# Linear attention and a gated feed-forward layer: turning the first chunks' keys and rows on TensorE, spreading the constants, halving the last store, and a new order

## The chip, the cores and the metric

The kernel runs on one core of one Trainium2 chip. The metric is the device time of one execution in microseconds (us); lower is better. The kernel before has a median of 525.44 us over three runs (525.37 to 525.9). The execution that the profiler recorded took 528.41 us, with 526.7 us between its first and its last instruction (its span). All rows below are from that execution.

Names used here: TensorE (PE in the profile, PEld for its weight loads) multiplies matrices; VectorE (DVE), ScalarE (ACT) and GpSimd (POOL) do elementwise work; SyncE (SP) issues nearly all DMA transfers. SBUF is the on-chip memory, PSUM the memory that TensorE writes.

## What is computed

For each of 4 batches and 8 heads, over 768 steps of 48 channels, in f32:

```python
for t in range(S):
    state = alpha[:, :, t, :, None] * state + np.einsum('bhd,bhe->bhde', k[:, :, t], v[:, :, t])
    y[:, :, t] = np.einsum('bhd,bhde->bhe', q[:, :, t], state)
```

The heads of a token are then laid side by side (3072 tokens of 384 numbers), and each token goes through a normalised, gated layer with d_ff = 1536:

```python
xn = x / np.sqrt(np.mean(x * x, axis=-1, keepdims=True) + 1e-06) * rms_g
g = xn @ w_gate
return ((g * (1.0 / (1.0 + np.exp(-g)))) * (xn @ w_val) @ w_out).astype(np.float32)
```

The weights arrive as 64-bit floats.

## The kernel before

**Splitting.** TensorE works on pairs of f16 numbers: each f32 operand is split into a high f16 part (ACT) and the remainder, the low part, also f16. A product is three matmuls, high by high, high by low and low by high (`SPLIT`, m = 0 to 2). The low part is made by DVE as a subtraction, or by TensorE, which subtracts the high part from a copy of the f32 value that lies in PSUM (a matmul with a matrix of -1 on the diagonal, `minus`), after which ACT copies the rest out. Which way is used for which chunk stands in the lists `LOW_A`, `LOW_X`, `LOW_K`, `LOW_V`, `LOW_W`.

**Chunks.** A chunk is 128 tokens of one batch; there are 24. Chunks 0 to 3 are the first of each batch. `attention(cc)` handles one: two scans on DVE (`scan`, L702) give the running decay, keys and queries are scaled by it (`kh`, `qp`, L720 and L725), TensorE forms the scores (L835 in f32 for the first chunks, L826 in f16 pairs for the others), DVE masks them (L841), they are split, and TensorE multiplies them with the values into `y` (L916). For the states the split keys are needed with tokens on the partitions, `kT`. The rows `y` are normalised with `rms_g` into `x`, split, and needed with channels on the partitions, `xT`.

**Turning.** Before, both turns are DMA transposes on the SP queue: `k_turn` (L736) and `x_turn` (L1013).

**Feed-forward.** The 24 chunks form the groups `GROUPS` = 4, 2, 2, 4, 4, 4, 4. For a group, `expert_in` runs over 12 tiles of 128 hidden units: 9 matmuls for the gate (`mm_f_c_0`) and 9 for the value (`mm_f_c_1`), all L1152; ACT takes the silu of the first, DVE multiplies (`h`, L1169), and the result is split (ACT, then DVE at L1182). `expert_out` (L1222) multiplies with `w_out`; DVE scales the result (L1236) and a store takes it out (L1240). For group 0 the first five hidden tiles are done with 256 columns, first for chunks 0 and 1 (`mm_f_0_*`), then for chunks 2 and 3 (`mm_f_2_*`), so that TensorE can begin before chunks 2 and 3 are normalised. The three PSUM buffers `mm` are shared by these products, the key products of chunks whose low part TensorE makes, and, for names in `BANK_M`, the weights that are decoded.

**Weights.** `decode` loads a weight tile of 64-bit floats into one of two buffers `raw`, and DVE and ACT make f32 words of it with integer operations (L525, L538, L530, L546, L557) and split them (ACT L562, DVE L565). For names in `LOW_W` the words are joined in PSUM in two halves (L578) and the low part is made by TensorE (L590) and ACT (L596).

**Order.** The program is not written in its order. Every step is an operation with a cost, an engine, its buffers and a due time; `Plan.order` places them with a simple model, and the tables `PACE`, `GAP`, `FIRST_DUE`, `AHEAD`, `STRIDE`, `LATE`, `NUDGE` and `HOLD` shift due times. Each engine then executes its own list strictly in that order.

**Constants.** Masks and diagonal matrices are made at the start by POOL (memset and affine_select).

## Time and profile before

| | us |
|---|---|
| median of three runs | 525.44 |
| the profiled execution | 528.41 |
| its span | 526.7 |
| PE busy | 501.4 |
| DVE busy | 401.5 |
| ACT busy | 277.2 |
| POOL busy | 27.1 |

Busy time is the union of an engine's instructions. Matmuls overlap, so the mean duration of one is longer than the distance between two. An instruction of DVE starts about 0.08 us before the one ahead of it has ended, so the sum of durations is a little more than the time they take. A wait is named by what released it. The clock of PE is given as the share of its full speed that was granted: 1.00 stands for 2.4 GHz, 0.50 for 1.2 GHz.

### The profile page before, as it was taken

The page shows a single profiled execution, that of the slowest core. Times are in us where ns is not written, and L with a number is a line of the kernel's source. Part 1 is how long each engine was busy: PE and PEld are TensorE (multiplying, and loading weights), DVE is VectorE, ACT ScalarE, POOL GpSimd, SP SyncE. Part 2 cuts the span into 40 slices and gives each one's busy share as a digit, 9 for nine tenths or more (in the row PEclk, how much of TensorE's full clock was granted, in tenths as well). Part 3 has the DMA queues.
Part 4 walks back from the last instruction along what each step waited for, and adds up shares of the span by engine and source line. Part 5 has one row for each costly group of instructions (what it writes and reads, how often), then busy time and mean ns, then how long its engine had stood idle before and what let it go on. Part 6 is the DMA issues. An engine that isn't in the chain of part 4 may idle for free.

```text
span 526.7 us, 11922 instructions
## 1 busy us (share of the span) xinstructions
PE 501.4 (95%) x4826; PEld 299.4 (57%) x4826; DVE 401.5 (76%) x755; ACT 277.2 (53%) x720; POOL 27.1 (5%) x61
## 2 busy tenths in 40 slices
PE   3768999999999999999999999999999999999995
PEld 2447744567877886444566445556544456444453
DVE  7999899999999999999988659999474631233330
ACT  3787776645554663546554567766575630233300
POOL 4001000010001000001100000101000000000000
PEclk9959899999999999999999999999999999999999
DMA  8989757437534245444267756525532201000000
GB/s 254 311 213 221 252 181 242 127 92 188 133 81 92 69 102 132 109 110 91 69 167 208 178 154 144 163 83 124 208 107 90 75 16 46 15 1 1 1 30 34
DMA packets 70669, 64.68 MB, mean 123 GB/s; under 512 B 39921, under 2 KB 64625, under 8 KB 70609
## 3 DMA queue, kind: packets, MB, share of 16 engines
q1 hardware_dynamic: 70464, 63.68, 45.1%
q8 instruction: 38, 0.62, 0.5%
q10 hardware_dynamic: 144, 0.20, 0.1%
q14 instruction: 23, 0.18, 0.1%
HBM read 49.84 MB, written 4.72 MB: 104 GB/s over the span
## 4 chain that ended last, share of the span: by engine, by line
PE 73%; DVE 16%; issue 2%; ACT 1%; DMA 1%; DVEq 0%
PE mm L1152 44%; PE mm_po L1222 21%; DVE dk L702 3%; PE at L826 2%; PE y L916 2%; PE y L906 2%; DVE h L1182 1%; DVE h L1169 1%; DMA xT<-x 1%; DVE at L841 1%; PE at L934 1%; DVE a L896 1%; DVE raw_o L530 1%; DVE wu_o L557 1%; DVE s L816 1%
## 5 line engine op out<-in xcount | busy, mean ns | idle before, releaser
L1152 PE MATMUL mm<-xT,wg 128*128 128x512 f16 (+1 forms) x1602 | 290.0, 340 | 2.5 <-DMA xT<-x 2.5
L1152 PEld LDWEIGHTS <-wg 128*128 128x128 f16 x1602 | 154.9, 98 | 122.9 <-issue 3.0
L1222 PE MATMUL mm_po<-wo,h 128*128 128x384 f16 x864 | 145.9, 326 | 1.1 <-DVE ob L1236 0.8
L1222 PEld LDWEIGHTS <-h 128*128 128x128 f16 x864 | 82.6, 98 | 55.5 <-issue 1.8
L1169 DVE SCALAR_TENSOR_TENSOR h<-mm,sl 128x512 f32<-128x512 f32 (+1 forms) x89 | 51.8, 582 | 44.3 <-PE mm L1152 42.7
L490 ACT ACTIVATE h<-h 128x512 f16<-128x512 f32 (+1 forms) x89 | 48.5, 545 | 68.1 <-DVE h L1169 67.6
L1163 ACT ACTIVATE sl<-mm 128x512 f32<-128x512 f32 (+1 forms) x89 | 45.4, 510 | 40.8 <-PE mm L1152 40.2
L1182 DVE TENSOR_TENSOR h<-h,h 128x512 f16<-128x512 f32 (+1 forms) x89 | 51.6, 581 | 17.7 <-ACT h L490 17.7
L702 DVE TENSOR_TENSOR_SCAN dk<-att,seed 112x520 f32<-112x520 f32 x48 | 60.5, 1260 | 2.5 <-DMA att<-att 2.0
L974 POOL TENSOR_TENSOR ss<-ss,mhalf 128x1 f32<-128x1 f32 x24 | 20.3, 846 | 400.9 <-DVE ss L964 355.0
L1236 DVE TENSOR_SCALAR ob<-mm_po 128x384 f32<-128x384 f32 x24 | 13.2, 551 | 31.5 <-PE mm_po L1222 31.5
L893 ACT CAST a<-at 128x512 f16<-128x512 f32 x48 | 27.6, 582 | 13.9 <-DVE at L841 13.4
L841 DVE TENSOR_TENSOR at<-at,mask 128x512 f32<-128x512 f32 x48 | 31.7, 691 | 0.7 <-PE at L835 0.5
L916 PE MATMUL y<-v,a 128*128 128x48 f16 x576 | 27.2, 186 | 0.1
L896 DVE TENSOR_TENSOR a<-at,a 128x512 f16<-128x512 f32 x38 | 25.1, 682 | 0.0
L645 ACT ACTIVATE wu_s<-wu_s 128x768 f32<-128x768 f32 x18 | 15.1, 840 | 15.6 <-DVE wu_s L641 15.6
L916 PEld LDWEIGHTS <-a 128*128 128x128 f16 x576 | 22.8, 98 | 0.4
L906 PE MATMUL y<-s,q 112*128 112x96 f16 x240 | 22.8, 204 | 0.0
L490 ACT ACTIVATE k<-kh 112x512 f16<-112x512 f32 x24 | 15.0, 625 | 11.6 <-DVE kh L720 8.9
L958 ACT ACTIVATE junk<-y 128x384 bf16<-128x384 f32 x24 | 11.7, 486 | 17.1 <-PE y L916 8.8
L826 PEld LDWEIGHTS <-k 48*128 48x128 f16 x480 | 13.5, 94 | 6.7 <-issue 6.3
L906 PEld LDWEIGHTS <-q 112*128 112x128 f16 x240 | 14.8, 96 | 4.1
(142 smaller groups left out, 447.9 us busy)
## 6 DMA issues: line engine op xcount, KB each, us to landing
att<-att SPq DMA_DIRECT2D x22, 675.9 KB, 5.7
v<-vtok SPq DMA_DIRECT2D x24, 192.0 KB, 3.9
raw_i<-w_gate SPq DMA_DIRECT2D x12, 384.0 KB, 4.4
raw_i<-w_val SPq DMA_DIRECT2D x12, 384.0 KB, 5.3
raw_o<-w_out SPq DMA_DIRECT2D x6, 768.0 KB, 4.9
raw_s<-w_gate SPq DMA_DIRECT2D x12, 384.0 KB, 3.6
raw_s<-w_val SPq DMA_DIRECT2D x12, 384.0 KB, 4.9
raw_s<-w_out SPq DMA_DIRECT2D x6, 768.0 KB, 4.6
```

Source lines behind the costliest of these rows:

```text
L490: nc.scalar.activation(dst, src, AF.Copy, scale=scale, accum_out=stat[:rows, col : col + 1])
L702: nc.vector.tensor_tensor_scan(out, x, start.rearrange("r g p c -> r (g p c)"), 0.0, op0=ALU.mult, op1=ALU.add)
L841: nc.vector.tensor_tensor(t["sc"][j], t["sc"][j], mask[:, int(not sc16)].to_broadcast([P, NP, C]), op=ALU.mult,)
L893: nc.scalar.copy(a_tile()[:, j, 0], t["sc"][j])
L896: nc.vector.tensor_tensor(a_tile()[:, j, 1], t["sc"][j], a_tile()[:, j, 0], op=ALU.subtract)
L906: nc.tensor.matmul(yps[:, 2 * p * D : 2 * (p + 1) * D], t["q16"][:, x, p, :], s16_tile()[:, y, p].rearrange("r j e -> r (j e)"), start=p = ...
L916: nc.tensor.matmul(yps[:, (2 * p + j) * D : (2 * p + j + 1) * D], a_tile()[:, j, x, p, :], t["v16"][:, y, p, j, :], start=first and p == 0 ...
L1152: nc.tensor.matmul(ps[:, :n], wg[:, f, x, j, kk, :], xT[:, y, kk, cs], start=i == 0, stop=i == 3 * NK - 1,)
L1163: nc.scalar.activation(t["sl"][:, :n], t[0][:, :n], AF.Silu, scale=1.0 / (S_X * S_W))
L1169: nc.vector.scalar_tensor_tensor(t["h"][:, :n], t[1][:, :n], S_H / (S_X * S_W), t["sl"][:, :n], op0=ALU.mult, op1=ALU.mult,)
L1182: nc.vector.tensor_tensor(h16_of(g, f)[:, 1, cs], t["h"][:, :n], h16_of(g, f)[:, 0, cs], op=ALU.subtract)
L1222: nc.tensor.matmul(t[i][:, :DM], h16_of(g, f)[:, x, ts], wo[:, f // 2, y, f % 2, :], start=f == 0 and m == 0, stop=f == NF - 1 and m == 2,)
```

## The change

For chunks 0 to 3 (`TURN_X`) the normalised rows are no longer split and then turned by a DMA transpose. DVE writes `x32`, TensorE turns it by three f32 matmuls against the identity `same` into the `y` bank (`x_bring`), ACT writes the high part straight into `xT`, and the low part comes from TensorE and ACT for chunks 0 and 1 (`LOW_X`) and from DVE for 2 and 3 (`xT_lo`). For chunks 0 to 2 (`TURN_K`, where scores are in f32) the keys are turned in the same way, by four f32 matmuls into an `mm` bank (`k_bring`), and the low part is made by TensorE and ACT. Chunk 3 is now in `SC16`: its scores are in f16 pairs, and its keys are split by DVE and turned by DMA, as before. The values of chunks 0 and 1 have their low part from DVE now, no longer from TensorE. The weight tile i1 joins `LOW_W`, and i1, i3 and i10 join `BANK_M`. POOL makes `minus` and two masks only; ACT derives `same`, `minus_w` and `plus_w` from `minus`; DVE clears `seed2`. The last store is in two halves of columns, one scaled by DVE and stored from SP, one scaled by ACT and stored from ACT. Costs and order tables are new, so all five lists differ.

```diff
-SC16 = []
+SC16 = [3]
-LOW_K = [0, 1]
-LOW_V = [0, 1]
-BANK_M = ["i0"]
+LOW_K = [0, 1, 2, 3]
+TURN_X = [0, 1, 2, 3]
+TURN_K = [0, 1, 2, 3]
+BANK_M = ["i0", "i1", "i3", "i10"]
-LOW_W = ["i0", "i6", "o1"]
+LOW_W = ["i0", "i1", "i6", "o1"]
...
-PACE = [0.932, 0.85, 1.174, 1.159, 0.85, 0.982, 1.687, 0.852]
+PACE = [0.973, 0.85, 1.174, 1.159, 0.85, 1.072, 1.687, 0.852]
...
-    nc.gpsimd.memset(seed2, 0.0)
+    nc.vector.memset(seed2, 0.0)
...
+    for x, scale in ((same, -1.0), (minus_w, 1.0 / S_W), (plus_w, -(2.0**128) / S_W)):
+        nc.scalar.activation(x, minus, AF.Copy, scale=scale)
...
         def k_bring():
-            t["kps"] = buf(ps_mm, [R, 512], F32, "mm", ("k", cc))
-            nc.tensor.matmul(
-                t["kps"], same[:R, :R], t["kh"].rearrange("r p c -> r (p c)"),
-                start=True, stop=False,
-            )
+            t["kps"] = buf(ps_mm, [P, 512], F32, "mm", ("k", cc))
+            for p in range(NP):
+                nc.tensor.matmul(
+                    t["kps"][:, p * R : (p + 1) * R], t["kh"][:, p, :], same[:R, :R],
+                    start=p == 0, stop=True, skip_group_check=True,
+                )
...
+        def gain_r():
+            t["x32"] = tl(ap, [P, DM], F32, "x32")
+            nc.vector.scalar_tensor_tensor(
+                t["x32"], t["y"][:, :DM], t["ss"][:, 3:4], rg, op0=ALU.mult, op1=ALU.mult
+            )
+
+        def x_bring():
+            for k in range(NK):
+                nc.tensor.matmul(
+                    t["y"][:, k * P : (k + 1) * P], t["x32"][:, k * P : (k + 1) * P], same,
+                    start=k == 0, stop=True, skip_group_check=True,
+                )
+
+        def xT_hi():
+            nc.scalar.copy(xT_part(0), xT_ps())
+
+        def xT_lo():
+            nc.vector.tensor_tensor(xT_part(1), xT_ps(), xT_part(0), op=ALU.subtract)
...
-        if cc in LOW_X:
-            xs = add("DVE", "xs", gain_at, [y1, rt, tiles["rg"]], [key("y"), key("ss")])
-            xd = add("ACT", "xh", x_hi_of, [xs], [key("y"), key("x16")])
-            xl = add("PE", "xless", x_less, [xd], [key("y"), key("x16")])
-            xl = add("ACT", "xr", x_rest, [xl], [key("y"), key("x16")])
+        if cc in TURN_X:
+            yk, xk = key("y"), ("xT", g)
+            x = add("DVE", "xs", gain_r, [y1, rt, tiles["rg"]], [yk, key("ss"), key("x32")])
+            xt = add("PE", "xid", x_bring, [x], [yk, key("x32")])
+            xt = add("ACT", "xh", xT_hi, [xt], [yk, xk])
+            if cc in LOW_X:
+                xt = add("PE", "xless", x_less, [xt], [yk, xk])
+                xt = add("ACT", "xr", x_rest, [xt], [yk, xk])
+            else:
+                xt = add("DVE", "xTl", xT_lo, [xt], [yk, xk])
...
             if ends(i):
-                op("ACT", 0.1, lambda i=i: store(i), [e], [o], due=now + 5)
+                for h, (e, q) in enumerate((("DVE", "SP"), ("ACT", "ACT"))):
+                    r = op(e, 0.3, lambda i=i, h=h: back(i, h), [tail[0]], [b, o], due=now + 2)
+                    op(q, 0.4, lambda i=i, h=h: store(i, h), [r], [o], due=now + 5)
```

POOL's list at the very start, before: `same`, `same_v`, `minus`, `minus_w` and `plus_w` are diagonal matrices.

```order
L446 AFFINE_SELECT mask<-mask 128x384
L459 MEMSET plus_w 128x128
L461 MEMSET minus_w 128x128
L463 AFFINE_SELECT minus<-minus 128x128
L463 AFFINE_SELECT minus_w<-minus_w 128x128
L463 AFFINE_SELECT plus_w<-plus_w 128x128
L463 AFFINE_SELECT same<-same 128x128
L463 AFFINE_SELECT same_v<-same_v 128x128
```

And POOL's list at the same place now, from `minus` on.

```order
L432 MEMSET minus 128x128
L440 MEMSET mask 64x128
L433 ISA
L433 AFFINE_SELECT minus<-minus 128x128
L441 MEMSET mask 64x128
L440 MEMSET mask 64x128
```

Six affine_selects have become two, the first of them earlier in the list.

DVE's list before, where chunk 3 is normalised (`x_3`); the first number in a name is the chunk, or for `h` group, hidden tile and chunk.

```order
L538 TENSOR_SCALAR wu_i_685<-raw_i_532 128x768
L978 TENSOR_TENSOR x_3_691<-y_594,rg 128x384
L707 RECIPROCAL seed_95<-dk_507 112x8
L1169 SCALAR_TENSOR_TENSOR h_0_0_0_706<-mm_0_0_1_642,sl_0_0_658 128x256
L1169 SCALAR_TENSOR_TENSOR h_0_1_0_708<-mm_1_0_1_675,sl_1_0_687 128x256
L546 SCALAR_TENSOR_TENSOR wu_i_685<-raw_i_532,wu_i_685 128x768
L1002 SCALAR_TENSOR_TENSOR x_3_710<-x_3_691,ss_655,x_3_710 128x384
```

And DVE's list now, where chunk 3 is normalised and the low parts of chunks 2 and 3 are written into `xT` (L969).

```order
L797 TENSOR_TENSOR sd_132<-st_131,gd_681 112x192
L537 SCALAR_TENSOR_TENSOR wu_i_749<-raw_i_581,wu_i_749 128x768
L810 TENSOR_TENSOR s_139<-sd_132,s_139 48x4x48
L948 SCALAR_TENSOR_TENSOR x_3_784<-y_598,ss_698,rg 128x384
L969 TENSOR_TENSOR xT_390<-y_502,xT_390 128x3x128
L556 SCALAR_TENSOR_TENSOR wg<-wu_i_749,wg 128x768
L810 TENSOR_TENSOR s_139<-sd_132,s_139 48x4x48
L529 TENSOR_SCALAR wu_i_805<-raw_i_713 128x768
L1149 SCALAR_TENSOR_TENSOR h_0_3_0_817<-mm_3_0_1_767,sl_3_0_762 128x256
L1162 TENSOR_TENSOR h_0_2_765<-h_0_2_0_753,h_0_2_765 128x256
L969 TENSOR_TENSOR xT_390<-y_598,xT_390 128x3x128
```

Before, the last row of chunk 3 is the 65th instruction of DVE after the first scan has begun, and a DMA follows; now it is the 81st, and the first gates `h` stand ahead of it in both.

DVE's list now a little earlier, between the decoding of two weight tiles and the first gate (`raw_i_408` holds i3, `raw_i_516` holds i4).

```order
L516 TENSOR_SCALAR raw_i_408<-raw_i_408 128x768
L521 SCALAR_TENSOR_TENSOR raw_i_408<-raw_i_408 128x768
L548 SCALAR_TENSOR_TENSOR wu_i_562<-raw_i_408 128x768
L693 SCALAR_TENSOR_TENSOR dk_578<-att_224,seed 112x520
L529 TENSOR_SCALAR wu_i_595<-raw_i_516 128x768
L556 SCALAR_TENSOR_TENSOR wg<-wu_i_562,wg 128x768
L698 RECIPROCAL seed_95<-dk_578 112x8
L1149 SCALAR_TENSOR_TENSOR h_0_0_0_677<-mm_0_0_1_568,sl_0_0_564 128x256
```

In both lists the first gate `h_0_0_0` stands behind the last step of i3 and the first step of i4; before, the first step of x_3 stood between them, and now the first scan of chunk 4 stands there instead, and the first steps of i3 directly ahead.

The SP queue before, from the first `xT` on.

```order
L1013 DMA_TRANSPOSE xT_476<-x_0_391 128x6x128
L1013 DMA_TRANSPOSE xT_476<-x_1_397 128x6x128
L736 DMA_TRANSPOSE kT_520<-k_2_494 128x8x112
L517 DMA raw_i_532<-w_gate 128x3x128
L517 DMA raw_i_532<-w_val 128x3x128
L517 DMA raw_i_637<-w_gate 128x3x128
L517 DMA raw_i_637<-w_val 128x3x128
L1013 DMA_TRANSPOSE xT_476<-x_2_592 128x6x128
```

The SP queue now, at the loads of i3 and i4.

```order
L508 DMA raw_i_408<-w_gate 128x3x128
L508 DMA raw_i_408<-w_val 128x3x128
L727 DMA_TRANSPOSE kT_468<-k_3_401 128x8x112
L508 DMA raw_i_516<-w_gate 128x3x128
L508 DMA raw_i_516<-w_val 128x3x128
L415 DMA v_544<-vtok 128x384
```

Of the eight transposes that chunks 0 to 3 sent through this queue one is left, the keys of chunk 3.

## Rows read from the trace of the kernel before

**Rows 1.** The page's part on engines: busy us, share of the span, instructions.

```profile
PE 501.4 (95%) x4826; PEld 299.4 (57%) x4826; DVE 401.5 (76%) x755; ACT 277.2 (53%) x720; POOL 27.1 (5%) x61
```

**Rows 2.** Busy time of each engine in stretches of the span: start and end, then length, PE, PEld, DVE, ACT and POOL busy with their instructions, the granted clock of PE, the share of the DMA engines and GB/s.

```profile
30.00:40.00 10.00, 6.70 (x153) 5.21 (x143) 9.96 (x16) 8.38 (x23) 0.72 (x1) 0.50 0.68 179
40.00:50.00 10.00, 10.00 (x135) 8.62 (x132) 9.87 (x21) 8.28 (x24) 2.20 (x1) 0.94 0.87 209
50.00:60.00 10.00, 7.45 (x53) 5.64 (x51) 8.40 (x17) 5.99 (x14) 0.00 (x0) 0.83 1.04 308
...
500.00:526.70 26.70, 21.19 (x130) 12.12 (x128) 5.69 (x19) 0.00 (x0) 0.00 (x0) 0.98 0.09 32
```

**Rows 3.** The same columns for the time from 62 us to 500 us.

```profile
62.00:500.00 438.00, 436.71 (x4221) 256.85 (x4220) 340.81 (x643) 235.03 (x616) 16.75 (x25) 1.00 0.41 110
```

**Rows 4.** The chain of work that ended last, in order of time: start, us, what.

```profile
45.99 0.60 DVE x L1002
...
47.13 6.43 DMA xT<-x
53.70 1.14 PE mm L1152 x9
...
55.40 5.37 PE mm L1152 x36
...
450.44 46.62 PE mm L1152 x216
```

**Rows 5.** The columns of rows 2 for three short stretches around the start of chunks 2 and 3 on PE.

```profile
51.10:53.70 2.60, 0.05 (x2) 0.04 (x2) 1.52 (x4) 0.51 (x3) 0.00 (x0) 1.00 1.19 227
53.70:58.20 4.50, 4.50 (x26) 3.20 (x27) 3.98 (x9) 3.80 (x8) 0.00 (x0) 0.62 0.97 331
58.20:65.80 7.60, 7.60 (x70) 6.73 (x69) 6.18 (x14) 5.53 (x17) 0.00 (x0) 1.00 0.63 199
```

**Rows 6.** The same columns for the stretch in which DVE goes from the first scan to the second scan of chunk 4.

```profile
3.60:54.30 50.70, 35.84 (x426) 24.47 (x427) 48.35 (x80) 35.78 (x91) 7.51 (x19) 0.87 0.98 260
```

**Rows 7.** Groups of DVE's instructions in that stretch: line, operation, out<-in, shapes, count, busy us, mean ns of one, idle before and what ended it.

```profile
L565 DVE SCALAR_TENSOR_TENSOR wg<-wu_i,wg 128x768 f16<-128x768 f32 x5 | 4.7, 941 | 0.0
...
L776 DVE SCALAR_TENSOR_TENSOR v<-v,v 128x384 f16<-128x384 f32 x5 | 2.6, 547 | 0.0
...
L557 DVE SCALAR_TENSOR_TENSOR wu_i<-raw_i 128x768 int32<-128x768 int32 x2 | 1.9, 953 | 0.0
...
L1182 DVE TENSOR_TENSOR h<-h,h 128x256 f16<-128x256 f32 x4 | 1.6, 407 | 0.0
L732 DVE TENSOR_TENSOR k<-kh,k 112x512 f16<-112x512 f32 x2 | 1.4, 679 | 0.0
L982 DVE SCALAR_TENSOR_TENSOR y<-y,ss,rg 128x384 f32<-128x384 f32 x2 | 1.2, 617 | 0.0
...
L578 DVE SCALAR_TENSOR_TENSOR mm_i<-raw_i,wu_i 128x384 int32<-128x384 int32 x2 | 1.0, 558 | 0.0
...
L953 DVE SCALAR_TENSOR_TENSOR st<-at,st 112x192 f32<-112x192 f32 x2 | 0.7, 350 | 0.0
```

**Rows 8.** The timeline of DVE at the start: start, us, instruction, in brackets the idle time before it and what ended it.

```profile
3.62 2.43 DVE L702 TENSOR_TENSOR_SCAN dk<-att,seed 112x520 f32<-112x520 f32 x1 [2.00 <-DMA att<-att]
...
6.40 1.24 DVE L702 TENSOR_TENSOR_SCAN dk<-att,seed 112x520 f32<-112x520 f32 x1
```

**Rows 9.** The timeline of POOL at the same time.

```profile
3.69 0.28 POOL L463 TENSOR_SCALAR_AFFINE_SELECT minus<-minus 128x128 f16<-128x128 f16 x1
...
4.67 0.29 POOL L463 TENSOR_SCALAR_AFFINE_SELECT same_v<-same_v 128x128 f32<-128x128 f32 x1
...
6.21 0.75 POOL L667 MEMSET s<- 112x768 f16 x1
```

**Rows 10.** Who waited for whom up to 62 us, DVE alone: total, times, longest.

```profile
DVE dk L702 <- DMA att<-att: 2.0, 1, 2.0
DVE wu_i L538 <- DMA raw_i<-w_val: 1.1, 1, 1.1
DVE at L841 <- PE at L835: 0.5, 1, 0.5
```

**Rows 11.** The view of the tile `raw_i` up to 60 us: its loads, from issue to landing.

```profile
DMA to landing us min/median/max: 3.3/5.5/9.3
```

**Rows 12.** The timeline of PE: the f32 product of chunk 1's keys with the identity, 512 columns.

```profile
16.69 1.33 PE L744 MATMUL mm_k<-kh,same 112*112 112x512 f32 x2
```

**Rows 13.** Two groups of ACT's instructions between 3.6 and 54.3 us, with the columns of rows 7.

```profile
L986 ACT CAST x<-y 128x384 f16<-128x384 f32 x2 | 1.0, 482 | 0.0
...
L1163 ACT ACTIVATE sl<-mm 128x256 f32<-128x256 f32 x5 | 1.9, 373 | 1.6 <-PE mm L1152 1.6
```

**Rows 14.** The end of the timeline.

```profile
521.23 0.56 DVE L1236 TENSOR_SCALAR ob<-mm_po 128x384 f32<-128x384 f32 x1 [5.29 <-PE mm_po L1222]
521.82 0.38 ACTq L1240 DMA_DIRECT2D out_dram<-ob  x1
```

**Rows 15.** The stores of the result from 495 us on, from issue to landing; the longest is the last, from ACT's queue.

```profile
DMA to landing us min/median/max: 1.8/1.9/3.1
```

More of the change, by code (lines that the diff above doesn't have):

```diff
@@ L78 @@
 WAIT = {"PE": 0.35, "DVE": 0.2, "ACT": 0.2, "POOL": 0.25}
[L79 to L94 removed]
+LOAD_LAG, LOAD_END, LOAD_RATE = 0.4, 1.5, 300.0
@@ new lines @@
+LOAD_SLOW = (0.0, 300.0)
+PACE = [0.973, 0.85, 1.174, 1.159, 0.85, 1.072, 1.687, 0.852]
+GAP = [0, 25.7, 24.9, -18.6, -16.6, 24.0, -5.2, 87.2]
+FIRST_DUE = [9.4, -38.4, -4.7, -34.8]
+AHEAD = [-1.5, 9.5, -2.5, 30.6, 29.3, 36.4, 14.8, -51.7]
+STRIDE = [-14.0, 30.1, 14.5, 23.2, 15.9, 12.3, 22.3, 48.8]
+LATE = dict(
+    abs=-155.3, al=2.5, claim=-33.2, gd=44.2, h=126.2, hl=27.7, join=-15.5, join2=-45.0,
+    k16=45.1, kTh=0.6, kTl=-19.8, kid=-2.4, kl=-124.4, kneg=-38.8, kr=-20.0, load=21.6,
+    mask=24.4, neg=-24.5, ob=-145.7, po=43.6, q16=72.8, ql=18.4, rec=-18.9, rest=-29.4,
+    sc=-20.0, scan=31.7, sd=3.7, sign=43.0, sl=-176.5, sq=-71.7, ss=-168.1, st=6.8, u=-52.8,
+    v16=13.6, vl=-29.7, wh=19.3, wh2=-22.9, wl=-119.8, wneg=17.3, x=12.6, x16=70.3, xTl=-28.9,
+    xh=-15.1, xid=33.7, xl=-109.3, xless=45.1, xr=73.9, xs=-90.7, y=-9.0, zero=-60.1,
@@ L444, in tile_attn_moe @@
         nc.gpsimd.memset(mask[rows, 1], a0 * S_QP)
-        nc.gpsimd.memset(mask[rows, 2], a0 * S_QP * S_V)
     nc.gpsimd.affine_select(
@@ L454, in tile_attn_moe @@
     )
-    minus = const.tile([P, P], F16, name="minus")
-    nc.gpsimd.memset(minus, 0.0)
+    same = const.tile([P, P], F32, name="same")
+    minus_w = const.tile([P, P], F16, name="minus_w")
     plus_w = const.tile([P, P], BF16, name="plus_w")
-    nc.gpsimd.memset(plus_w, 0.0)
-    minus_w = const.tile([P, P], F16, name="minus_w")
-    nc.gpsimd.memset(minus_w, 0.0)
-    for x, value in ((minus, -1.0), (minus_w, -1.0 / S_W), (plus_w, 2.0**128 / S_W), (same, 1.0), (same_v, S_V)):
-        nc.gpsimd.affine_select(
-            x, x, pattern=[[1, P]], compare_op=ALU.not_equal, fill=value, base=0,
-            channel_multiplier=-1,
-        )
+    for x, scale in ((same, -1.0), (minus_w, 1.0 / S_W), (plus_w, -(2.0**128) / S_W)):
+        nc.scalar.activation(x, minus, AF.Copy, scale=scale)
+    eps = const.tile([P, 1], F32, name="eps")
+    rare = const.tile([P, 1], F32, name="rare")
     for h, rows in enumerate((slice(0, HC), slice(HC, P))):
@@ L1092, in attention @@
+        ins = [key("a16"), key("v16"), key("y")] + ([] if first else [key("q16"), key("s16")])
+        y0 = add("PE", "y0" if first else "y", lambda: output(0), [l0, l1, vl, sl], ins)
+        y1 = add("PE", "y0" if first else "y", lambda: output(1), [y0], ins)
         sq = add("ACT", "sq", square, [y1], [key("y")])
@@ L1231, in ends, with cols, back, store @@
             return g == len(GROUPS) - 1 and t0 + i == GROUPS[g] - 1
-        def back(i):
-            ob = buf(mp, [P, DM], F32, "ob", f"{g}_{t0 + i}")
-            t["ob", i] = ob
-            nc.vector.tensor_scalar_mul(ob, t[i][:, :DM], 1.0 / (S_H * S_W))
-        def store(i):
+        def cols(h):
+            return slice(0, DM) if h is None else slice(h * DM // 2, (h + 1) * DM // 2)
+        def back(i, h=None):
+            if not h:
+                t["ob", i] = buf(mp, [P, DM], F32, "ob", f"{g}_{t0 + i}")
+            x, y = t["ob", i][:, cols(h)], t[i][:, cols(h)]
+            if h:
+                nc.scalar.mul(x, y, 1.0 / (S_H * S_W))
+            else:
+                nc.vector.tensor_scalar_mul(x, y, 1.0 / (S_H * S_W))
+        def store(i, h=None):
             o0 = src(chunks[i]) * C
-            (nc.scalar if ends(i) else nc.sync).dma_start(out[o0 : o0 + C, :], t["ob", i])
+            (nc.scalar if h else nc.sync).dma_start(
+                out[o0 : o0 + C, cols(h)], t["ob", i][:, cols(h)]
+            )
         n = len(chunks)
```

165 lines of the change are left out of this document (56 added, 109 removed).

## The prediction

> **What bounds the kernel now.** The page's part on engines comes first: PE is busy for 95% of the span, no other engine over 76% [rows 1]. So the question is where PE is not busy, or is slow. The busy time by stretches answers it. From 62 to 500 us PE lacks 1.3 us of 438 [rows 3]; nothing that leaves its work alone can gain more there. In the last stretch 5.5 us are missing, nearly all after the last matmul [rows 2]. The rest is in the first 60 us: 3.3 us idle from 30 to 40 us, at half clock, and 2.55 us idle from 50 to 60 us at 0.83 of the clock [rows 2].
>
> In those first 60 us DVE is the engine that is never idle: 9.96 us of 10, 9.87 of 10 [rows 2], and from its first scan to the second scan of chunk 4 it is busy for 48.35 us of 50.7, with 80 instructions [rows 6]. The chain of waits shows how this reaches PE: DVE ends the low part of x_3 at 46.6 us, its transfer takes 6.43 us, and at 53.70 us PE begins the first matmuls of chunks 2 and 3 [rows 4]. PE has by then stood still for 2.55 of 2.60 us, and after that its granted clock is 0.62 on average for the next 4.5 us, then 1.00 again [rows 5].
>
> What decides is therefore the moment at which PE can begin chunks 2 and 3 (the transition; 53.70 us before), whether PE idles just before it, and the tail. After the transition PE has the same work in both kernels, but for small things below.
>
> **The change, part by part.**
>
> *DVE's work up to the transition.* Counted to the same place, the second scan of chunk 4, the list has 79 instructions before it and now 83. Added: one low part of a value tile, 0.55; one low part of the queries of chunk 3, bounded by the keys of the same shape, 0.68; two halves of i1's words, 2 x 0.56; four small state steps of chunk 4 that have been brought forward, each at most the 0.35 of the state step in the rows, of which I take 1.1 in all (two work on 48 rows, and the smallest does four columns). Gone: one low part of keys 0.68, one of a weight tile 0.94, one joining of words 0.95, one low part of h 0.41 [rows 7]. Normalising takes six instructions in both: four of 0.62 and two of about 0.6 against two of 0.62, two of 0.55 and two of 0.60, within 0.2 us. Sum: 3.45 - 2.98, +0.5 us of DVE.
>
> *The first scan.* It takes 2.43 us, the next one 1.24 [rows 8], both reading the same amount. Beside the first POOL runs five affine_selects (3.69 to 4.96 us), beside the second only a memset, and that scan is not longer for it [rows 9]. Now there are two affine_selects, ahead of most memsets, and by the same durations they end before 3.6 us. The gain lies between 0 (a first scan is slow anyway) and 1.2 us; I take 1.2, since the second scan shows that POOL's memsets alone do no harm. The Trainium skill ("SBUF — State Buffer", section "Who interferes with whom") says that a DVE instruction with two inputs in SBUF is blocked by a GpSimd instruction that reads SBUF and not by one that only writes; the rows agree, 2.43 beside affine_selects and 1.24 beside a memset. The copies of the diagonals go to ACT, which waits for DVE at that time anyway; four or five instructions below 0.5 us before the first keys exist.
>
> *Waits of DVE.* Of the 50.7 us it is idle for 2.35, of which 1.1 is one wait for a load of weights and 0.5 one for the scores [rows 6, 10]. Now DVE is more often behind ACT: following the new lists by hand with these durations, the low parts of i2, i3 and i5 and of the value tile of chunk 4 stand behind ACT copies for 0.3 to 1 us each, 2.0 us in all, and the last gate ahead of the scan and two state steps wait another 1.0. Bounds: 0 and twice that. The load that cost 1.1 us has more room, since seven of eight transposes have left the queue. So the list ends where it did: +0.5 - 1.2 + (3.0 - 2.35) = -0.05, the second scan of chunk 4 at 54.2 us.
>
> *The turn on TensorE.* In place of 6.43 us of transfer [rows 4] chunk 3 now has three f32 matmuls of 128 columns, at most the 1.33 us of 512 columns [rows 12], an ACT copy of 0.48 [rows 13], and a subtraction on DVE of about 0.6. But x_3 now comes later in DVE's list: its last step is the 81st and no longer the 65th instruction. Only a gate and a state step, 0.8 us, stand between it and the second scan, so it ends at 53.4 us: the transfer's 6.4 us have been spent on DVE work that was moved ahead. What is late next is DVE itself. The range is 50.4 (no waits at all) to 57.6 (all waits double, no gain at the scan).
>
> *PE around the transition.* Now it still has the second half of the last tile of chunks 0 and 1, nine matmuls of 256 columns. They wait for the buffer that the gate of the fourth tile frees, and that gate stands two instructions (0.6 and 0.41) ahead of the end at 53.4: 52.4 us. 46.62 us for 216 matmuls of 512 columns [rows 4] are 0.216 each, so 1.0 us for the nine; then 48 small state matmuls (0.5), one `minus` matmul (0.2) and two of 384 columns that claim the bank for i6 (0.3). The first matmul of chunks 2 and 3 starts at 54.4 to 54.5, +0.8 against 53.70. The two claims came behind the start before, which gives back 0.3. So the transition alone is a loss of 0.5 us.
>
> *The clock.* Before, 4.5 us at a mean clock of 0.62 followed on the standstill [rows 5]; at full clock the same work takes 4.5 x 0.62 = 2.8, so 1.7 us were lost. Now PE's gaps before the transition are shorter (about 1.9 us at one place, the last tile of 1.0 us between that gap and the start). I take the dip as avoided: -1.7. The bounds are 0 and -1.7.
>
> *PE's work after the transition.* One chunk's state matmuls are left over in both. The three f32 products of x, the four of the keys and the f16 scores of chunk 3 all fall before 54 us, where DVE is the bound. Nothing to add. The rest of the list is reordered; PE has no room there, and DVE has 97 us of room in 438 [rows 3] but almost none before 250 us. I take 0, bounded by -1.3 (all of PE's gaps closed) and +1.5 (the same again).
>
> *The tail.* The last scaling takes 0.56 us and its store is issued 0.03 us later [rows 14]. Halves of 192 columns take at most ACT's 0.37 for 256 columns [rows 13], so the stores go out 0.2 us earlier. They land 3.1 us after the issue from ACT's queue, against 1.8 to 1.9 from SP's [rows 15]; one half still goes through ACT, so at most 0.3 more is gained by half the bytes. I take -0.3 in all; bounds 0 and -0.5 (with the SP landing time for both it would be -1.4, which the ACT half excludes).
>
> **Sum.** +0.5 - 1.7 + 0 - 0.3 = -1.5 us on the profiled execution, 526.7 to 525.2 in span, 528.41 to 526.9 in time. That execution is 2.97 us above the median of the runs; carried to the median, 525.44 - 1.5 = 523.9.
>
> **The rivals.**
>
> *No change: DVE's list sets everything, and the dip stays.* DVE's work to the transition is the same within 0.5 us, for which the count above speaks; if PE's idle 1.9 us are enough to lower the clock again, only -0.3 + 0.5 is left: 525.6, or 525.2 with a little less waiting. Against it: after the gap PE has more than 2 us of work before the transition, where before it had none.
>
> *Slower: DVE stops at the first step of i4, and PE with it.* The load of i4 needs the buffer of i1, which is free only when i1's halves are joined. Counted back from 53.4, i4's first step lies 26 instructions, 12.3 us of work and 1.2 of waits earlier, at 39.9, and the end of that joining nine more, 5.5 and 0.5, at 33.9. Behind that step in DVE's list stand the low part of i3 and the first gate, which alone frees an `mm` buffer; one of the other two is held by the keys of chunk 2 until after the transition. From a landing time of 6.0 us on, PE waits for the load. The median is 5.5, the longest 9.3 [rows 11]: at 9.3 the transition comes 3.3 us later, and the dip returns with it: 523.9 + 3.3, or + 5.0, so 527 to 529. For it: DMA is 98% busy in that stretch [rows 6]. Against it: fewer transfers now.
>
> *More gained: no waits.* If DVE's 2.0 us behind ACT fall away, the last low part ends at 51.4 and the transition 2.0 us earlier, and the reordering closes half of PE's gaps: 523.9 - 2.0 - 0.6, some 521.5. Against it: ACT is 36 us busy in the stretch and copies stand right ahead of DVE's steps.
>
> *The page's rule does nothing here.* If the first scan stays at 2.43, all of DVE's list is 1.2 us later: 525.1, no measurable change; it is counted with the first rival.
>
> **How the numbers follow.** A measurement of this kernel tells no change from a change within 0.2%, 1.05 us. The forecast (its own range 522.8 to 525.0) has 0.42, of which 0.12 is within that bound. No change has 0.26; slower by the load of i4 has 0.18, of which 0.01 stays within the bound; more gained 0.14. Faster 0.30 + 0.14 + 0.01 (from no change), same 0.12 + 0.24 + 0.01, slower 0.17 + 0.01: 0.45, 0.37, 0.18. The range of 8 in 10 takes in half of the two outer cases: 521.2 to 527.6.
>
> **What the profile after would show.** Right: a first scan near 1.24 us; no DMA wait of PE before chunks 2 and 3, whose first matmul starts between 53 and 55.5 us; a granted clock of 1.00 in the 5 us after it; 62 to 500 us as full as before. Wrong: DVE waiting for `raw_i` for more than 2 us with PE idle behind it; a clock near 0.6 after the transition; more than 3 us of PE idle after 62 us, which would be the new order's own doing.

## The result and the profile after

The kernel after takes 528.3 us in the median (527.02 to 530.96, eight runs) against 525.85 us for the kernel before, measured beside it (525.37 to 526.52, eight runs). The ratio is 1.0053, with a 95% interval of 1.0031 to 1.0075. It is slower by 2.5 us; the prediction was 523.9 with a range of 521.2 to 527.6.

The profiled execution of after took 530.96 us, with a span of 529.2 (before 528.41 and 526.7): the same 2.5 us. The busy time of PE answers to [rows 1] and has hardly moved, 502.3 against 501.4 us:

```profile
PE 502.3 (95%) x4877; PEld 303.8 (57%) x4877; DVE 400.9 (76%) x758; ACT 277.5 (52%) x728; POOL 19.0 (4%) x50
```

So again the question is where PE stands still, and again it is the first 60 us. The windows of after, in the columns of [rows 2] (busy time of PE, PEld, DVE, ACT and POOL with counts, granted clock, DMA share, GB/s):

```profile
8.00:14.00 6.00, 4.56 (x25) 3.67 (x25) 5.17 (x8) 2.00 (x8) 0.00 (x0) 1.00 1.05 224
...
40.00:50.00 10.00, 8.06 (x118) 6.38 (x118) 8.46 (x16) 7.24 (x19) 1.27 (x2) 0.85 0.70 207
...
58.20:62.70 4.50, 4.50 (x43) 4.02 (x42) 4.50 (x10) 4.46 (x16) 0.00 (x0) 1.00 0.44 106
62.00:500.00 438.00, 436.69 (x4229) 257.96 (x4228) 342.39 (x645) 234.57 (x617) 12.89 (x25) 1.00 0.44 112
```

The last row is [rows 3] again, 436.69 against 436.71: nothing was won or lost there. The third row begins with the start of chunks 2 and 3 (shown below), and its clock is 1.00, where [rows 5] had 0.62. The clock is lower ahead of it: 0.85 on average from 40 to 50 us, and within that 0.50 from 47.0 to 50.4 us, after PE had stood still for 1.83 us. The first row has a partner in before that the rows ahead of the prediction do not show:

```profile
8.00:14.00 6.00, 5.48 (x21) 3.15 (x22) 5.81 (x9) 2.88 (x10) 0.00 (x0) 1.00 1.05 307
```

With the same share of busy time, 1.05, the DMA engines delivered 307 GB/s before and 224 after.

The timeline of PE of after around the transition (the start of chunks 2 and 3):

```profile
46.71 5.76 PE L1132 MATMUL mm<-xT,wg 128*128 128x256 f16 x36 [1.83 <-DVE h L1149]
...
58.04 0.32 PE L563 MATMUL y_i<-minus 128*128 128x384 f16 x1 [0.33 <-DVE xT L969]
58.20 2.02 PE L1132 MATMUL mm<-xT,wg 128*128 128x256 f16 x17
```

The transition comes at 58.20, 4.5 us later than in [rows 4]. From there to the last scaling (58.20 to 523.40) after needs 465.20 us, before 467.53 (53.70 to 521.23); and the tail is 0.33 us longer. 4.50 - 2.33 + 0.33 = 2.5: the whole difference of the spans.

Why the transition is late stands in the waits of DVE up to 70 us (in total, times, longest), which answer to [rows 10]:

```profile
DVE dk L693 <- DMA att<-att: 2.6, 2, 1.7
DVE wu_i L529 <- DMA raw_i<-w_val: 2.5, 2, 1.4
DVE kh L711 <- DMA att<-att: 1.6, 1, 1.6
```

and in its timeline at the start ([rows 8]):

```profile
3.79 1.24 DVE L693 TENSOR_TENSOR_SCAN dk<-att,seed 112x520 f32<-112x520 f32 x1 [1.74 <-DMA att<-att]
...
5.31 1.24 DVE L693 TENSOR_TENSOR_SCAN dk<-att,seed 112x520 f32<-112x520 f32 x1
8.17 0.69 DVE L711 TENSOR_TENSOR kh<-att,dk 112x512 f32<-112x512 f32 x1 [1.62 <-DMA att<-att]
```

The first scan takes 1.24 us instead of 2.43, and then `kh` waits 1.62 us for the second half of chunk 0 and starts at 8.17, later than before:

```profile
7.68 0.69 DVE L720 TENSOR_TENSOR kh<-att,dk 112x512 f32<-112x512 f32 x1
```

Over the stretch of [rows 6], from the first scan to the second scan of chunk 4, DVE is busy for 47.77 us of 54.71:

```profile
3.79:58.50 54.71, 38.76 (x476) 29.29 (x477) 47.77 (x84) 36.59 (x97) 3.24 (x6) 0.91 0.85 226
```

The chain of waits of after begins with transfers, where that of before [rows 4] named one transfer at the transition; these are its longest pieces up to 51 us:

```profile
2.20 8.11 DMA att<-att
10.32 9.12 DMA raw_i<-w_val
21.40 9.39 DMA raw_i<-w_val
38.89 5.84 DMA raw_i<-w_val
46.71 3.77 PE mm L1132 x18
```

The four transfers are second 1 (the large half of chunk 1) and the second loads of i1, i2 and i4. SP issued that of i1 when second 1 had landed (10.30 us), and that of i2 when i1 had been worked on. Second 0, for which `kh` waits, is not in the chain. The 18 matmuls run while the clock is low: 3.77 us, where 18 of the same shape take 2.13 later in the same execution.

What the new order did to those transfers is in the queue: chunks 0 and 1 are each loaded in two halves, a small one (112 x 521, what the scans read) and a large one (112 x 1024, what `kh` and `qp` read besides). Before, SP issued first 0, second 0, first 1, second 1; after, it issues first 0, first 1, second 0, second 1. The issue times of these four are the same within 0.01 us. The landing times, read from the trace, in us (the last two columns are the second loads of weight tiles i0 and i1):

| kernel | first 0 | second 0 | first 1 | second 1 | chunk 2 | i0 | i1 |
|---|---|---|---|---|---|---|---|
| before | 3.52 | 5.13 | 5.92 | 8.05 | 11.97 | 14.22 | 16.67 |
| after | 3.69 | 8.08 | 4.37 | 10.30 | 14.94 | 17.16 | 19.44 |

Up to i1 the queue holds the same bytes, and they are 2.8 us late at the end. The later loads are also issued later: i1's first load at 8.09 us, once second 0 had landed, where before it went out at 5.94. Behind i1 the order differs again. Two loads of values now stand ahead of the load of chunk 3, which is issued at 14.95 and lands at 24.49 (before: 9.00 and 19.14).

The tail of after, against [rows 14]:

```profile
523.40 0.36 DVE L1223 TENSOR_SCALAR ob<-mm_po 128x192 f32<-128x192 f32 x1 [5.29 <-PE mm_po L1202]
523.78 0.33 SPq L1227 DMA_DIRECT2D out_dram<-ob  x1
523.79 0.33 ACT L1221 ACTIVATE ob<-mm_po 128x192 f32<-128x192 f32 x1 [22.62 <-DVE ob L1223]
524.15 0.38 ACTq L1227 DMA_DIRECT2D out_dram<-ob  x1
```

ACT's half starts when DVE's is done, so the last store is issued 0.75 us after the scaling begins; before it was 0.59.

### The profile page after: what moved, and what is told of

It reads as the page before. It is cut to its first block, busy times and chain, and to the rows that moved or that the text cites. A ratio compares the mean times of both kernels' runs of the same rounds, so it can differ in the third digit from the quotient of the medians.

```text
span 529.2 us, 11987 instructions
## 1 busy us (share of the span) xinstructions
PE 502.3 (95%) x4877; PEld 303.8 (57%) x4877; DVE 400.9 (76%) x758; ACT 277.5 (52%) x728; POOL 19.0 (4%) x50
## 4 chain that ended last, share of the span: by engine, by line
PE 88%; DMA 7%; DVE 3%; ACT 1%; issue 0%; SPq 0%; DVEq 0%
PE mm L1132 52%; PE mm_po L1202 27%; DMA raw_i<-w_val 5%; PE at L820 3%; PE y L882 2%; PE y L872 2%; PE at L900 2%; DMA att<-att 2%; DMA kT<-k 1%; DVE wu_i L537 0%; DVE wg L556 0%; DVE mm_i L569 0%; DVE wu_i L529 0%; SPq L410 0%; DVE at L835 0%
## 5 line engine op out<-in xcount | busy, mean ns | idle before, releaser
L693 DVE TENSOR_TENSOR_SCAN dk<-att,seed 112x520 f32<-112x520 f32 x48 | 59.2, 1234 | 3.0 <-DMA att<-att 2.6
L1223 DVE TENSOR_SCALAR ob<-mm_po 128x384 f32<-128x384 f32 (+1 forms) x24 | 13.0, 543 | 34.8 <-PE mm_po L1202 34.7
L940 POOL TENSOR_TENSOR ss<-ss,mhalf 128x1 f32<-128x1 f32 x24 | 14.5, 607 | 412.1 <-DVE ss L930 376.9
L481 ACT ACTIVATE v<-v 128x384 f16<-128x384 f32 x24 | 12.5, 523 | 13.2 <-PE at L900 7.4
L481 ACT ACTIVATE k<-kh 112x512 f16<-112x512 f32 x21 | 13.1, 625 | 10.1 <-DMA kT<-k 5.7
L820 PE MATMUL at<-q,k 48*128 48x128 f16 x504 | 17.9, 217 | 0.0
```

The source lines that it names most:

```text
L481: nc.scalar.activation(dst, src, AF.Copy, scale=scale, accum_out=stat[:rows, col : col + 1])
L693: nc.vector.tensor_tensor_scan(out, x, start.rearrange("r g p c -> r (g p c)"), 0.0, op0=ALU.mult, op1=ALU.add)
L820: nc.tensor.matmul(o, t["k16"][r, x, p, :], t["q16"][r, y, p, :], start=p == 0 and m == 0, stop=m == 2, skip_group_check=True,)
```

## The experiments

In the diffs, `steps` is the planned list of operations and `put(a, b)` moves operation a directly behind b; `loads[c]` are the loads of chunk c, `raw_loads[n]` that of weight tile n; the comments are added here. All ratios are to the kernel before, run on the same chip in the same rounds.

**again, swap, late_att, both.** The first theory had two suspects: the order of chunk 0's and chunk 1's halves, and the loads of chunks 4 and 5, which stand ahead of weight tiles that are needed sooner.

```diff
+put(loads[1][0], loads[0][1])          # swap, both
+put(loads[4][0], raw_loads["i2"])      # late_att, both
+put(loads[5][0], raw_loads["i3"])      # late_att, both
```

The kernel after, unaltered:

> The changed kernel once more, unaltered, to see how steady its landings are. Theory L (late loads): the second half of chunk 0's data lands near 8 us again, the load of i2 near 30.8 us, DVE waits for loads for 4 to 5 us between its first scan and 58 us, and PE begins chunks 2 and 3 at 57.5 to 58.5 us; ratio 1.004 to 1.007 to the kernel before. Rival C (chance): the slow transfers of the first 14 us were an accident of that one execution; then the second half of chunk 0 lands before 6.5 us, the transition comes before 56 us, and the ratio stays the same only if something else costs the time.

Measured: 528.29 us (524.9 to 531.39, 12 runs; before 526.15), ratio 1.0034 (1.0013 to 1.0056). The loss is there again, and so are the late loads: in the profiled execution second 0 lands at 7.88 us, i2 at 34.15 and the transition comes at 59.50, both later than theory L had put them. Rival C, chance, falls.

The halves in the old order:

> The second half of chunk 0's data is issued ahead of the first half of chunk 1's, as before the change; nothing else differs. Theory L: the keys of chunk 0 start at about 6.7 us and not at 8.17, so DVE is 1.5 us earlier up to 24 us; what is left of it at the transition depends on the loads of chunk 3 and i2, whose landing is set by the bytes ahead of them, so 0 to 1.5 us, 0.5 expected. Rival W (the new work of DVE, ACT and PE is what makes the transition late): no change at the transition, DVE waits for ACT and PE in place of the load.

Measured: 525.20 us, ratio 0.9989 (0.9967 to 1.0011): 3.1 us less than the kernel after beside it, more than either theory had asked of it. The loss is gone with one load moved by one place. The runs of swap fall into two groups, seven from 523.72 to 525.46 us and five from 527.14 to 527.89; by means instead of medians the difference is 2.5 us. The profiled execution, at 527.75, is one of the five.

Chunks 4 and 5 loaded later:

> The loads of chunks 4 and 5 (676 KB each, needed after 42 us) are issued behind those of i2 and i3; nothing else differs. Theory L: the load of i2 lands about 2.5 us earlier (28.3), chunk 3's about 1 us earlier, DVE's waits of 0.85 and 1.36 us go, the transition comes at 56 to 56.5 and the time falls by 1.5 to 2.2 us against the changed kernel. Rival W: the waits for loads go but come back as waits for ACT or PE; transition after 57.5, time within 0.5 us of the changed kernel.

Measured: 529.90 us, ratio 1.0067 (1.0041 to 1.0093). A miss: not faster, if anything slower.

Both edits:

> Both moves of loads together. Theory L: waits for loads in the first 58 us fall from 5.0 to about 1.1 us (the load of i4 is left), the transition comes at 54.5 to 55.5, the time falls by 3 to 4 us against the changed kernel, to 0.997 or 0.998 of the kernel before. Rival W: transition after 57, time within 1 us of the changed kernel.

Measured: 528.05 us, ratio 1.0029 (1.0009 to 1.0049). A miss as well: the second edit takes back what the first had won.

Why, the timeline of PE shows. In late_att:

```profile
46.32 2.08 PE L1137 MATMUL mm<-xT,wg 128*128 128x256 f16 x9 [3.17 <-DVE h L1154]
```

and in both:

```profile
43.98 2.29 PE L1137 MATMUL mm<-xT,wg 128*128 128x256 f16 x10 [3.07 <-DVE h L1154]
```

PE waits 3.1 us for a gate of DVE, and DVE has waited for tile i4 (2.5 and 2.3 us). The load of chunk 5, moved behind i3, now stood ahead of i4 in the queue: in both it was issued at 31.86 and landed at 39.32, and i4, issued at 34.30, landed at 42.00. That is the mechanism of the prediction's rival (DVE stops at the first step of i4), made by the experiment itself. The nine or ten matmuls then take 2.1 to 2.3 us, where nine take 1.14 at full clock: after the standstill the granted clock is lower (0.66 in both from 40 to 50 us).

What swap changed, in its window from 8 to 14 us, in its timeline of DVE and in that of PE:

```profile
8.00:14.00 6.00, 4.35 (x26) 3.43 (x26) 4.60 (x7) 2.38 (x8) 0.00 (x0) 1.00 1.06 285
```

```profile
3.71 1.24 DVE L697 TENSOR_TENSOR_SCAN dk<-att,seed 112x520 f32<-112x520 f32 x1 [1.65 <-DMA att<-att]
...
6.50 0.69 DVE L715 TENSOR_TENSOR kh<-att,dk 112x512 f32<-112x512 f32 x1
```

```profile
45.04 4.09 PE L1137 MATMUL mm<-xT,wg 128*128 128x256 f16 x36 [1.06 <-DVE h L1154]
...
55.29 1.91 PE L1137 MATMUL mm<-xT,wg 128*128 128x256 f16 x16
```

`kh` starts at 6.50 with no wait, the DMA engines deliver 285 GB/s, and the transition comes 2.9 us earlier than in after. The loads behind are only partly back: chunk 2 lands at 13.59 and i1 at 18.35 us, between the two rows of the table of landings. The 36 matmuls take 4.09 us, in after 5.76, where the clock had fallen. Two explanations are left for the loss: the late second half itself, or the slower transfers behind it.

**before_seq.** The order alone, put into the kernel before.

```diff
+put(loads[0][1], loads[1][0])
```

> The kernel before, with one thing of the change: the second half of chunk 0's data is issued behind the first half of chunk 1's (the order of the kernel after), nothing else. Theory O (that order is what costs, whatever the rest): the second half lands about 8 us instead of 5.13, the DMA engines deliver 205 to 235 GB/s from 8 to 14 us instead of 307, the loads behind land 2 to 3 us later, the transition comes 2 to 3 us after 53.70, and the time is 1.004 to 1.006 of before. Rival S (the order only costs where the first scan is short; with the scan of 2.43 us DVE would not be ready for it anyway, and later loads have slack): kh starts at most 0.7 us later, ratio 1.000 to 1.0015.

Measured: 526.76 us against 526.10, ratio 1.0011 (0.9996 to 1.0027). The landing times are those of after (second 0 at 8.15, chunk 2 at 14.94, i1 at 20.25), and so is the rate:

```profile
8.00:14.00 6.00, 4.92 (x20) 2.89 (x21) 5.57 (x8) 2.80 (x9) 0.00 (x0) 1.00 1.06 233
```

So the order by itself makes the transfers slow, as theory O had it, with nothing else of the change present. The time follows rival S, though a loss of up to 1.4 us lies within the interval: the kernel before can bear the order. `kh` starts at 8.24 instead of 7.68, and in the profiled execution the transition is at 53.91. One reason is seen in the trace: the first step of i2 comes at 33.85 us, when that load has landed (32.89), while DVE in after asks for it from 29.5 us on.

**mirror.** Which part of the order slows the transfers?

```diff
+put(loads[0][1], loads[1][1])          # in the kernel after: first 0, first 1, second 1, second 0
```

> The kernel after with one thing altered: chunk 0's second half is issued behind BOTH halves of chunk 1, so that chunk 1's halves stand next to each other and chunk 0's do not (first 0, first 1, second 1, second 0). It tells what of the order slows the transfers. Theory A (halves of one chunk next to each other go fast): about half of the loss in rate is regained, 250 to 275 GB/s from 8 to 14 us. Theory B (what slows is that both small first halves go ahead of both large second halves): 200 to 235 GB/s as in the kernel after. In both kh starts later still, at 9 to 10.5 us, and the time is 1.004 to 1.009 of before.

Measured: 529.10 us, ratio 1.0053 (1.0034 to 1.0072), and

```profile
8.00:14.00 6.00, 3.33 (x20) 3.17 (x22) 4.05 (x6) 1.96 (x7) 0.00 (x0) 1.00 1.05 218
```

Theory B: with both small first halves ahead the transfers are slow, whichever second half follows. (In all slow orders the two large halves also stand next to each other; no run separates these two readings.) The run bears on the two explanations of swap as well. Here `kh` waits longer than in after:

```profile
9.83 0.69 DVE L715 TENSOR_TENSOR kh<-att,dk 112x512 f32<-112x512 f32 x1 [3.41 <-DMA att<-att]
```

It starts 1.7 us later than in after, and yet the time is that of after (1.0034 and 1.0053). Where these 1.7 us go is seen at the first step of i2, here in after, mirror and swap:

```profile
30.89 0.56 DVE L529 TENSOR_SCALAR wu_i<-raw_i 128x768 int32<-128x768 int32 x1 [1.36 <-DMA raw_i<-w_val]
...
30.51 0.56 DVE L531 TENSOR_SCALAR wu_i<-raw_i 128x768 int32<-128x768 int32 x1 [0.93 <-DMA raw_i<-w_val]
...
29.38 0.56 DVE L531 TENSOR_SCALAR wu_i<-raw_i 128x768 int32<-128x768 int32 x1 [1.45 <-DMA raw_i<-w_val]
```

In all three DVE waits for the load, and mirror is no later there than after: up to this point a longer wait of `kh` costs nothing, and the landing of i2 sets the pace. With the chain of waits of after, which leaves out second 0, this speaks for the lateness of the loads behind. It does not show it to the end, because the profiled execution of mirror is one of the quickest of its ten (527.25 us): DVE waits for no load behind i2, and the transition comes at 55.47, close to swap's.

**swap_pool.** Is the short first scan worth what the prediction gave for it? In swap, the constants go back to POOL.

```diff
-nc.vector.memset(seed2, 0.0)
+nc.gpsimd.memset(seed2, 0.0)
...
-    nc.scalar.activation(x, minus, AF.Copy, scale=scale)
+    nc.gpsimd.memset(x, 0.0)
+    nc.gpsimd.affine_select(x, x, ..., fill=value, base=0, channel_multiplier=-1)
```

> The kernel with chunk 0's halves in the old order, with the constants same, minus_w and plus_w made by POOL again instead of ACT, and the second seed cleared by POOL instead of DVE. Theory F (the first scan is slowed by POOL's constants beside it, and what it loses is mostly given back in the wait of 1.37 us for v that follows): the first scan takes 2.2 to 2.5 us instead of 1.24, the transition comes 0 to 0.5 us after 55.29, ratio 0.998 to 1.000 of before. Rival N (the whole 1.2 us goes through DVE's list to the transition, as the prediction had it): transition 56.3 to 56.6, ratio 1.001 to 1.002.

Measured: 524.39 us, ratio 0.9976 (0.9958 to 0.9995), and the premise fell: the first scan still took 1.24 us. The timelines of DVE and of POOL in that kernel:

```profile
3.68 1.24 DVE L701 TENSOR_TENSOR_SCAN dk<-att,seed 112x520 f32<-112x520 f32 x1 [2.06 <-DMA att<-att]
```

```profile
3.65 0.20 POOL L455 MEMSET plus_w<- 128x128 bf16 x1
3.81 1.20 POOL L456 TENSOR_SCALAR_AFFINE_SELECT minus_w<-minus_w 128x128 f16<-128x128 f16 x1
4.97 0.29 POOL L456 TENSOR_SCALAR_AFFINE_SELECT plus_w<-plus_w 128x128 bf16<-128x128 bf16 x1
```

This time POOL lost: its affine_select took 1.20 us instead of 0.29 and ended when the scan did. So the run does not answer what a scan of 2.43 us would cost here. It does show that making these constants on ACT and DVE instead of POOL gains nothing that can be measured.

**pool2.** The same kernel once more.

> The kernel swap_pool a second time, unaltered. If making the constants on POOL is worth something against the swapped kernel (0.9976 against 0.9989, intervals that overlap), it comes again below 0.9985; if it is worth nothing, 0.9985 to 0.9995, where the swapped kernel was. Either way not slower than the swapped kernel by the 1.2 us that the prediction gave to the constants. The first scan is 1.24 us if it begins ahead of POOL's affine_select and that one is held up (1.2 us instead of 0.29), or 2.4 if POOL is first.

Measured: 524.93 us, ratio 0.9988 (0.9969 to 1.0006), where swap was. The scan is again 1.24 us and POOL's affine_select 1.22.

**late_i4.** What is left between swap and an earlier transition: the waits for i2 (1.4 us) and i4 (0.5). On top of swap, chunk 4 goes behind i2, chunk 5 this time behind i4; and each half of the last store gets its own tile.

```diff
+put(loads[1][0], loads[0][1])
+put(loads[4][0], raw_loads["i2"])
+put(loads[5][0], raw_loads["i4"])
...
-x, y = t["ob", i][:, cols(h)], t[i][:, cols(h)]
+y = t[i][:, cols(h)]
+x = ob1 if h else t["ob", i][:, cols(h)]
```

> The kernel with chunk 0's halves in the old order, and besides: the loads of chunks 4 and 5 issued behind the third and the fifth block of w_in (i2 and i4), and the two halves of the last store in tiles of their own. Theory W (the waits for i2, 1.4 us, and i4, 0.5 us, are what holds the transition at 55.29 in the swapped kernel): i2 lands by 25 us, i4 by 41 us, both waits go, the transition comes at 53.0 to 54.0 us, ratio 0.995 to 0.997 of before. Rival P (TensorE's waits for xT and wg bind, not DVE's list): the transition stays at 55.0 to 55.6, ratio 0.998 to 1.000. Tail, theory T (ACT's half waits for DVE's half only because they share a tile): ACT's scaling starts within 0.15 us of DVE's, and end less start of the scaling is 5.4 to 5.5 us instead of 5.80. Rival (they share the source in PSUM, so they still go one after the other): 5.75 to 5.85.

Measured: 525.17 us, ratio 0.9988 (0.9969 to 1.0006). In the profiled execution (524.21 us) no wait of DVE for a weight tile is left:

```profile
DVE dk L698 <- DMA att<-att: 1.7, 1, 1.7
DVE seed L425 <- PEq L1466: 1.0, 1, 1.0
DVE v L775 <- ACT v L481: 0.4, 1, 0.4
```

and the transition is at 51.79, earlier than theory W asked. But the median over 12 runs is that of swap: on the median the edit brought nothing that these runs can tell. The tail answers to its rival: tiles of their own do not help, ACT's half still starts behind DVE's.

```profile
517.05 0.33 ACT L1228 ACTIVATE ob<-mm_po 128x192 f32<-128x192 f32 x1 [22.62 <-DVE ob L1230]
```

What the halves still share is the bank in PSUM that both read. That this is the reason was not tried.

**best, best2.** swap_pool with chunk 4 behind i2 and chunk 5 behind i4, twice.

> Chunk 0's halves in the old order, the constants same, minus_w and plus_w and the second seed by POOL, chunk 4 loaded behind i2 and chunk 5 behind i4. Theory W (what the transition still waits for are the loads i2 and i4, in the executions whose transfers are slow): no wait of DVE for raw_i before 50 us, transition at 51.5 to 53 us, the slow half of the executions goes, 523.5 to 524.5 us, ratio 0.995 to 0.9975. Rival (late loads bring nothing in the time, as late_i4 at 0.9988 against the swapped kernel at 0.9989 suggests): 0.9975 to 0.999.

Measured: 524.74 us, ratio 0.9977 (0.9960 to 0.9995).

> The kernel best a second time, unaltered, since it is the best of several that were tried and part of its lead may be chance. If the lead is real: ratio 0.996 to 0.9985 again, with an interval below 1. If it was chance: 0.9985 to 1.000. By the trace: span less transition 470.0 to 470.8 us as in every kernel with the new program.

Measured: 525.00 us against 526.57, ratio 0.9965 (0.9948 to 0.9983). Both intervals lie below 1: this version is faster than the kernel before by 0.2 to 0.35%, and than the kernel after by 0.6 to 0.9%, going by the ratios. That the later loads add to this is not shown: swap_pool without them has 0.9976 and 0.9988. Theory W holds only in part: the profiled executions of both still show DVE waiting for weight tiles, 3.0 and 1.4 us in all; 1.76 us of best are a wait for i5, which now has chunk 5 ahead of it. The same transfer is not always equally fast: chunk 5's load, issued at 36.6 us in late_i4 and in best, took 5.27 us in the one execution and 7.50 in the other, and the second load of i5 behind it 5.34 and 8.05.

All profiled executions together, in us; the transition is the first matmul of chunks 2 and 3 behind the last wait:

| kernel | GB/s, 8 to 14 us | transition | span | span less transition |
|---|---|---|---|---|
| before | 307 | 53.70 | 526.7 | 473.0 |
| before_seq | 233 | 53.91 | 525.3 | 471.4 |
| after | 224 | 58.20 | 529.2 | 471.0 |
| again | 206 | 59.50 | 529.6 | 470.1 |
| late_att | 215 | 57.64 | 528.1 | 470.5 |
| mirror | 218 | 55.47 | 525.5 | 470.0 |
| swap | 285 | 55.29 | 525.8 | 470.5 |
| both | 264 | 56.50 | 526.9 | 470.4 |
| late_i4 | 282 | 51.79 | 522.3 | 470.5 |
| swap_pool | 294 | 52.20 | 522.4 | 470.2 |
| pool2 | 320 | 51.60 | 521.9 | 470.3 |
| best | 316 | 55.15 | 525.6 | 470.5 |
| best2 | 319 | 54.13 | 524.4 | 470.3 |

Single executions of one kernel lie up to 6.5 us apart (the runs of again go from 524.9 to 531.39), so a row is not the median of its kernel. The rate falls into two groups by the order of the halves, and the last column hardly scatters in the new program. The rate alone does not set the transition of a single execution: mirror with 218 GB/s and best with 316 have it at 55.47 and 55.15.

## Why the prediction was wrong

**What bounds the kernel: right.** The transition decides. In all eleven profiled executions of the new program the span less the transition lies between 470.0 and 471.0 us; nearly all of the spread between them, 521.9 to 529.6, comes ahead of it.

**DVE's work up to the transition: right.** Predicted from [rows 6]: 48.35 + 0.5 - 1.2 = 47.65 us. The trace of after has 47.77 us between the first scan and the second scan of chunk 4.

**The first scan: right in size, its worth not shown.** It went from 2.43 to 1.24 us. But in after the 1.2 us did not reach the next step: `kh` had to wait 1.62 us for its data. The runs with the constants on POOL again do not settle what it is worth, because their first scan was short too.

**Waits of DVE: the step that failed.** The prediction gave 3.0 us of waiting in this stretch, all of it behind ACT, and let the loads cost nothing ("has more room, since seven of eight transposes have left the queue"). The trace has 54.71 - 47.77 = 6.9 us, of which 5.0 behind loads: `kh` 1.6, chunk 3's scan 0.85, i2 1.36, i4 1.13. The whole is 3.9 us more than predicted, against 3.7 by which the transition missed (+4.5 instead of +0.8). Behind ACT it is only 0.7 us, and 0.8 behind PE. The prediction listed the transposes that left SP's queue and did not price the load that the new order moved within it, the second half of chunk 0, one place back. swap undoes that one move and gets 3.1 us back, and before_seq shows that the move alone slows the transfers. That their lateness, rather than the wait of `kh`, is what costs is argued from the chain of waits of after and from mirror, where `kh` is later still and the time the same; no run makes `kh` late alone. Not every wait comes from that move: the execution of swap still has 2.1 us behind loads, 1.45 of them for i2.

**The turn on TensorE, PE around the transition: right.** DVE's last low part of x_3 ends at 57.99 and PE starts the chunks at 58.20; DVE had become the last link, as the prediction said, but 4.6 us later than its 53.4.

**The clock: right behind the transition, wrong ahead of it.** The granted clock stays at 1.00 behind the transition, where before it fell to 0.62. Together with the claims that no longer follow the start, the way from the transition to the last scaling is 2.33 us shorter; -1.7 and -0.3 had been predicted. But a dip was not avoided: the clock fell to 0.50 from 47.0 to 50.4 us, after the 1.83 us in which PE waited for a gate that stood behind i4. 18 matmuls on the chain of waits took 3.77 us instead of 2.13, and DVE's 0.8 us behind PE fall here. This is a second term that the prediction had at nothing; in this trace it follows on the late load of i4. The other executions fit: in after, late_att, both and best2 slow matmuls follow on the wait for i4 and DVE waits for PE behind them; again, swap and mirror have neither slow matmuls there nor such a wait of DVE.

**PE's work after the transition: right,** 436.69 us of 438.

**The tail: wrong in sign,** -0.3 predicted, +0.33 in the profiled execution. The halves run one behind the other. From the start of the scaling to the end it takes 5.4 to 5.9 us with halves (eleven executions) and 5.3 and 5.5 whole (two), so there is no gain and a loss of some 0.2 us, within the scatter of one store's landing.

**The rivals.** The measured time lies where the rival "DVE stops at the first step of i4" put it, 527 to 529, and its mechanism is there: DVE waits 1.13 us for i4 and PE 1.83 us for the gate behind it. DVE came to that step 5.7 us after i4's buffer was free (the rival had 6.0), and the load landed after 6.7. The dip of the clock came with it, though ahead of the transition and not behind it. But the wait for i4 is 1.1 of the 5.0 us behind loads, and DVE came to it at 43.7 us, 3.8 later than the rival had counted; that its sum fits the measured time is in part luck. In late_att and both the wait for i4 was 2.5 and 2.3 us.

Without the moved load (swap), the ratio is 0.9989, -0.6 us with an interval from -1.7 to +0.6: the sum's -1.5 lies inside, no change does too.

## What to carry to other kernels

When a change writes the order anew, lay the two lists of every queue that issues transfers side by side for the first microseconds too, and price each transfer that has moved by what now lands late behind it; whoever shortens the first step of an engine must see that its next input is there. A load moved behind an urgent one must be looked at against the next urgent one as well: chunk 5 behind i3 stood in the way of i4, and behind i4 it stood ahead of i5, for which DVE waited 1.76 us in best and not at all in late_i4. Where two spans differ, measure one fixed mark (here the transition) in all kernels: what lies behind it may be the same to a microsecond, as it was here in the eleven executions of the new program.
